# Attention over halves of 64 positions, two units per set, in front of two matrix products

## The chip, the cores and the metric

One core of a Trainium2 chip runs the kernel. TensorE multiplies matrices into PSUM (8 banks), VectorE (DVE), ScalarE (ACT) and GpSimd (POOL) work element by element, and SyncE (SP) issues transfers, as ACT and POOL can too. Each engine takes its instructions in the order of the program and waits at an instruction until its semaphores are there. The metric is the device time in microseconds (us), the median of several runs; the profile is one execution, taken by the hardware profiler.

## The reference, cut to what matters

```python
batch, n_heads, seq, head_dim = (4, 8, 768, 64)      # q, k, v, float32; lam: one decay rate per head
for b in range(nb):                                   # nb = 12 blocks of 64 positions
    intra = np.einsum('bhic,bhjc->bhij', qb, kb) * Dmask[None]      # lam ** (i - j) where i >= j
    intra = np.einsum('bhij,bhjd->bhid', intra, vb)
    inter = np.einsum('bhid,bhde->bhie', qb * lam_pow[None], kv_state)
    out[:, :, sl] = intra + inter
    kv_state = lam_block[None, :, None, None] * kv_state + np.einsum('bhsd,bhse->bhde', kb * rev_pow[None], vb)
x = out.transpose(0, 2, 1, 3).reshape(3072, 512)
h = x @ w_in                                          # 512 -> 2048
return (h * sigmoid(h)) @ w_out                       # 2048 -> 512
```

## The kernel before

The 3072 rows are 24 units of 128 positions: unit u is batch u // 6, block u % 6, and all 8 heads (4 pairs). Per unit there are three loads of 256 KB (k, q, v, in runs of 64 floats, 256 bytes). The first `EARLY = 8` units load all three plainly through SP's queue (line 313), cast k and q to bf16 on DVE or ACT (`cast`) and turn them with eight TensorE transposes (line 402) and a copy out of PSUM (`kqT`). The other sixteen load k and q by casting transfers that POOL issues (line 316) and turn them by a transposing transfer in SP's queue (line 416).

The attention of a unit on TensorE has four parts:

- `score` (line 427): per pair and head one matmul with 64 rows of contraction, 128 columns of weights and 128 columns streamed, over the whole 128 x 128 square of positions. DVE multiplies by a triangle on the way out of PSUM (`st`, two instructions).
- `state` (line 446): k times scaled v, 128 rows, 64 columns of weights, 64 columns streamed. DVE and POOL add the carried state and scale it (`y`, `xe`, `xf`).
- `out_mm` (line 481) with `xe` and `kqT`: the carried part, 64 x 64 weights per head, 128 columns streamed.
- `out_mm` with `vd` and `st`: the own part, 128 rows, 64 columns of weights, 128 columns streamed. DVE scales the sum by powers of lam into `xt` (bf16).

The powers of lam are split: v carries lam ** (64 - position), the result lam ** (position - 64), so that the mask is a plain triangle of ones.

`product1` (line 518) multiplies `w_in` by `xt` in groups of 1, 2 or 4 units, that is 128, 256 or 512 columns streamed, four matmuls for each of 16 column blocks; ACT applies the Silu from a full bank. `product2` (line 552) adds 16 matmuls of 512 columns per unit, or of 2 x 256 for the first six units and the last one. Results leave through ACT or DVE and ACT's queue.

The order on every engine comes from `Planner`: each piece of work is a task with a key, a cost per engine, dependencies and buffers; a simulated clock starts the ready task with the smallest key whose buffers are free. Each matmul pair is a task of its own, so products stand between the parts of a unit's attention. `BEGIN` says when each engine is taken to be free of its constants (POOL 3.4, ACT 6.0). The planner's times only decide the order that is written into the program; at run time the semaphores decide. Weights are loaded in eight pieces of 1 MB by POOL, and the order of the start is written out:

```python
    sequence = "u0 i0 i1 u1 i2 u2 i3 u3 u4 u5 u6 o0 o1 u7 o2 o3".split() + [f"u{u}" for u in range(EARLY, NU)]
```

Before a piece of weights POOL copies one element of the preceding unit's k (`gated`, line 293), and so waits for its landing.

Of the kernel before, what the change touches and what calls it, by code (L numbers as in the profile page):

```python
# [25 lines left out]
class Buf:  # L26

    __slots__ = ("pool", "slot", "left", "tile", "with_")

    def __init__(self, pool, with_=None):  # L30
        self.pool, self.slot, self.left, self.tile, self.with_ = pool, None, 0, None, with_

SMALL, CAST, LARGE, HALF, TURN = (256, 16.4, 18.5), (256, 14.0, 31.0), (2048, 92.0, 92.0), (1024, 58.0, 58.0), (1024, 46.0, 46.0)


class Planner:

# [17 lines left out]
    def order(self):  # L59
# [63 lines left out]
        while len(out) < len(self.tasks):  # L123
# [9 lines left out]
            for e in free:  # L133
# [7 lines left out]
                kept, took = [], None  # L141
                while ready[e]:
# [7 lines left out]
                    if any(len(self.pools[p]) < n for p, n in need.items()):  # L150
                        kept.append((key, i, t))
                        continue
# [37 lines left out]
def kernel(  # L190
# [20 lines left out]
    EARLY = 8  # L211
# [6 lines left out]
    POOLS = dict(bank=8, raw=9, rv=4, kq=6, kqT=5, vd=4, st=3, xe=3, y=3, xf=3,  # L218
                 xt1=4, xt2=2, xt4=2, g=40, osb=3, osh=4, one=4, two=2, att=5)
# [3 lines left out]
    def tile_of(b, shape, dt, name):  # L223
# [3 lines left out]
        return b.tile  # L227

# [18 lines left out]
    tri_e = const.tile([128, U], F32, name="tri_e")  # L247
    nc.gpsimd.memset(tri_e, 1.0)
    nc.gpsimd.affine_select(
        out=tri_e, in_=tri_e, compare_op=AL.is_ge, fill=0.0,  # L250
        base=0, pattern=[[1, U]], channel_multiplier=-1,
    )
# [12 lines left out]
    lam_be = const.tile([128, NP], F32, name="lam_be")  # L265
    nc.scalar.activation(lam_v, log_all, AF.Exp, scale=pose[:, 0:1])
    for a in range(NP):
        nc.scalar.activation(lam_xe[:, a, :], row, AF.Exp, scale=log_lam[:, a:a + 1])
    nc.scalar.activation(lam_be, log_lam, AF.Exp, scale=float(U))
    w_in_bf = const.tile([128, KI, DFF], BF16, name="w_in_bf")  # L270
# [12 lines left out]
    def mult(e, o, a, b):  # L283
        (nc.vector if e == "DVE" else nc.gpsimd).tensor_tensor(o, a, b, op=AL.mult)  # L284

    gate = const.tile([128, 8], F32, name="gate")

    def gated(key, load, i, tile):

        t = add(key, {"POOL": 0.15}, lambda e: nc.gpsimd.tensor_copy(gate[:, i:i + 1], tile()), deps=[load],  # L293
                prior=pool_last[-1:])
        pool_last.append(t)

    pool_last = []

    def pool_load(key, w, fn, bufs, nbytes, kind, late=0.0):
        t = add(key, {"POOL": w}, fn, bufs=bufs, nbytes=nbytes, kind=kind, prior=pool_last[-1:], late=late)  # L300
        pool_last.append(t)
        return t
# [309 lines left out]
```

## Time and profile before

| | |
|---|---|
| time, median of 3 runs | 233.99 us (233.22 to 235.63) |
| span of the profiled execution | 231.6 us, 2.4 us under the median |
| TensorE busy | 212.2 us, 92% |
| DVE, ACT, POOL busy | 89.4, 82.7, 41.3 us |
| first product matmul, first uninterrupted products | 16.8 us, 20.9 us |
| scores, states, outputs on the chain that ended last | 2.7%, 2.8%, 6.6% of the span |
| products on that chain | 38.3% and 35.7% |

The span runs from the first to the last instruction. The page's slices give the busy tenths of each engine in 40 equal parts of it; the chain that ended last is followed back from the last instruction to what released it; a group's line gives its count, busy time, the mean of one, and what ended the idle time before it. Matmuls overlap in the pipeline, so the mean of one (some 0.2 us) says little of its cost; the steps from one start to the next do, and the chain shows those.

### The profile page before, as it was taken

The numbers are of one execution on the slowest core, as the hardware profiler recorded it, in microseconds if no ns is written. First come the engines' busy times: TensorE is split into PE (matmuls) and PEld (weight loads), VectorE is DVE, ScalarE is ACT, GpSimd is POOL, SyncE is SP. The second block draws the span as 40 slices with busy tenths as digits, with TensorE's granted clock in tenths as the row PEclk, the third lists the DMA queues.
The fourth block names the chain that finished last, engine by engine and source line by source line (L and its number), as shares of the span: only waits on it lengthen the run. The fifth ranks groups of instructions, "written<-read, shape, count | busy, mean of one in ns | idle before, by whom it ended". The sixth has DMA issues, their size and how long they took to land.

```text
span 231.6 us, 4583 instructions
## 1 busy us (share of the span) xinstructions
PE 212.2 (92%) x1950; PEld 134.5 (58%) x1968; DVE 89.4 (39%) x165; ACT 82.7 (36%) x149; POOL 41.3 (18%) x61
## 2 busy tenths in 40 slices
PE   0547889999999999999999999999999999999994
PEld 0336778878888884686754444444444444444453
DVE  1445285766130007555574663556542111110100
ACT  5431625684433221242521146522323333333221
POOL 3403014922240003350333341011100000000000
PEclk9999979999999999999999999999999999999999
DMA  5999999999999985999999999610101111001112
GB/s 120 203 196 232 217 211 216 167 185 182 159 174 197 152 228 67 195 120 147 167 146 195 193 157 172 123 48 0 48 3 42 48 48 45 14 31 48 73 63 91
DMA packets 102677, 29.67 MB, mean 128 GB/s; under 512 B 92544, under 2 KB 100480, under 8 KB 102656
## 3 DMA queue, kind: packets, MB, share of 16 engines
q0 software_dynamic: 39552, 8.39, 41.3%
q1 hardware_dynamic: 58496, 14.68, 37.8%
q10 hardware_dynamic: 4608, 6.30, 7.9%
q8 instruction: 15, 0.25, 0.4%
q14 instruction: 6, 0.05, 0.1%
HBM read 27.27 MB, written 6.29 MB: 145 GB/s over the span
## 4 chain that ended last, share of the span: by engine, by line
PE 87%; DMA 6%; SPq 2%; DVE 1%; ACT 1%; issue 1%
PE h_ps L518 38%; PE o_ps L552 36%; PE x_ps L481 7%; DMA raw<-in_v_dram 6%; PE d_ps L446 3%; PE st_ps L427 3%; SPq L313 2%; PE tr L402 1%; DVE xt L284 1%; ACT g L532 0%; DVE vd L284 0%; ACT kqT L277 0%; ACT kq L277 0%; DVE xe L284 0%; DVE kqT L279 0%
## 5 line engine op out<-in xcount | busy, mean ns | idle before, releaser
L518 PE MATMUL h_ps<-xt,w_in_bf 128*128 128x128 bf16 (+2 forms) x700 | 115.9, 290 | 1.1 <-DVE xt L284 0.6
L552 PE MATMUL o_ps<-w_out_bf,g 128*128 128x512 bf16 (+1 forms) x482 | 105.4, 330 | 0.7 <-issue 0.5
L532 ACT ACTIVATE g<-h_ps 128x512 bf16<-128x512 f32 x96 | 56.6, 598 | 95.9 <-PE h_ps L518 91.6
L518 PEld LDWEIGHTS <-w_in_bf 128*128 128x128 bf16 x704 | 60.4, 102 | 27.0 <-issue 1.1
L552 PEld LDWEIGHTS <-g 128*128 128x128 bf16 x496 | 47.5, 98 | 32.3
L284 DVE TENSOR_TENSOR st<-st_ps,tri_e 128x512 bf16<-128x512 f32 x48 | 30.9, 685 | 32.1 <-PE st_ps L427 32.1
L279 DVE COPY osb<-o_ps 128x512 f32<-128x512 f32 (+1 forms) x11 | 6.8, 619 | 54.7 <-PE o_ps L552 53.0
L316 POOL DMA_DIRECT2D kq<-in_k_dram x16 | 14.1, 883 | 61.8 <-PE x_ps L481 56.3
L277 ACT ACTIVATE osb<-o_ps 128x256 f32<-128x256 f32 (+1 forms) x20 | 9.6, 479 | 36.0 <-PE o_ps L552 31.0
L284 DVE TENSOR_TENSOR xt<-x_ps,lam_xe 128x512 bf16<-128x512 f32 x24 | 16.5, 688 | 6.3 <-PE x_ps L481 5.9
L402 PE MATMUL tr<-ident,kq 128*128 128x128 bf16 x64 | 7.3, 242 | 11.4 <-POOL gate L293 5.7
L284 DVE TENSOR_TENSOR vd<-raw,lam_v 128x512 bf16<-128x512 f32 x24 | 16.2, 683 | 2.9 <-DMA raw<-in_v_dram 2.9
L316 POOL DMA_DIRECT2D kq<-in_q_dram x16 | 14.2, 890 | 7.3 <-DMA w_out_bf<-in_moe_w_out_dram 6.3
L458 DVE TENSOR_TENSOR y<-d_ps,xf 128x256 f32<-128x256 f32 x16 | 6.8, 425 | 18.5 <-PE d_ps L446 18.5
L277 ACT ACTIVATE kqT<-tr 128x512 bf16<-128x512 bf16 x14 | 8.4, 597 | 11.0 <-PE tr L402 10.9
L284 POOL TENSOR_TENSOR xf<-y,lam_be 128x256 f32<-128x256 f32 x6 | 3.7, 611 | 47.9 <-DVE y L458 47.9
L402 PEld LDWEIGHTS <-kq 128*128 128x128 bf16 x64 | 4.5, 106 | 12.6 <-DVE kq L279 9.3
L427 PE MATMUL st_ps<-kqT 64*128 64x128 bf16 x192 | 10.2, 229 | 1.6 <-ACT kqT L277 0.9
L481 PE MATMUL x_ps<-kqT,xe 64*64 64x128 bf16 x160 | 11.1, 231 | 0.0
L481 PE MATMUL x_ps<-st,vd 128*64 128x128 bf16 x192 | 11.0, 235 | 0.0
L427 PEld LDWEIGHTS <-kqT 64*128 64x128 bf16 x192 | 6.0, 98 | 8.4 <-issue 7.8
L446 PE MATMUL d_ps<-vd,kq 128*64 128x64 bf16 x160 | 9.0, 209 | 1.5 <-DVE vd L284 1.5
(32 smaller groups left out, 55.3 us busy)
## 6 DMA issues: line engine op xcount, KB each, us to landing
raw<-in_v_dram SPq DMA_DIRECT2D x24, 256.0 KB, 6.3
out_dram<-osb ACTq DMA_DIRECT2D x17, 256.0 KB, 2.1
raw<-in_k_dram SPq DMA_DIRECT2D x8, 256.0 KB, 4.9
raw<-in_q_dram SPq DMA_DIRECT2D x8, 256.0 KB, 6.2
w_in_bf<-in_moe_w_in_dram POOLq DMA_DIRECT2D x4, 512.0 KB, 8.0
w_out_bf<-in_moe_w_out_dram POOLq DMA_DIRECT2D x4, 512.0 KB, 13.8
kq<-in_k_dram POOLq DMA_DIRECT2D x16, 128.0 KB, 5.2
kq<-in_q_dram POOLq DMA_DIRECT2D x16, 128.0 KB, 6.5
```

The source lines that it names most:

```text
L277: nc.scalar.activation(o, i, AF.Copy)
L279: nc.vector.tensor_copy(o, i)
L284: (nc.vector if e == "DVE" else nc.gpsimd).tensor_tensor(o, a, b, op=AL.mult)
L316: nc.gpsimd.dma_start(out=tile_of(kq, [128, 2, H, 64], BF16, "kq")[:, i], in_=src[i])
L402: nc.tensor.transpose(t[:, m, :], kq_of()[:, i, 2 * m:2 * m + 2, :], ident)
L427: nc.tensor.matmul(t[:, m, :], lhsT=t_of()[r, 0, m, :], rhs=t_of()[r, 1, m, :], start=True, stop=True)
L446: nc.tensor.matmul(t[r, m, :], lhsT=kq_of()[:, 0, 2 * m + h, :], rhs=vd.tile[:, 2 * m + h, :], start=True, stop=True)
L458: nc.vector.tensor_tensor(tile_of(src, [128, NP, 64], F32, "y"), d_ps.tile, xf[0].tile, op=AL.add)
L481: nc.tensor.matmul(t[r, m, :], lhsT=lhsT(h, r), rhs=rhs(h, r), start=first, stop=True, skip_group_check=True)
L518: nc.tensor.matmul(t[:, j, :], lhsT=w_in_bf[:, ko, 128 * m:128 * m + 128], rhs=xt[gi].tile[:, ko, :], start=(ko == 0), stop=(ko == KI - 1))
L532: nc.scalar.activation(tile_of(g, [128, per, n], BF16, "g"), bank.tile, AF.Silu)
L552: nc.tensor.matmul(t, lhsT=g.tile[:, j, 128 * gp:128 * gp + 128], rhs=w_out_bf[:, ko, cs], start=(ko == 0), stop=(ko == KO - 1))
```

## The change

- Work goes by sets: two batches at the same block of 128 positions (`SETS`, 12 sets; unit u is now block u // 4, batch u % 4). Each load of a set is one transfer of 512 KB in SP's queue. No load is cast by POOL; all k and q are cast on DVE or ACT.
- The first two sets (`PAIRED`) are loaded with two neighbouring positions in a row of 64 partitions per batch, in runs of 512 bytes, and have code of their own (`prepare_2`, `first_2`, `second_2`) with masks `tri_2` and powers `lam_v2`. The first four sets are turned by TensorE, the other eight by one transposing transfer each.
- Inside a unit attention goes by halves of 64 positions: the scores of the two diagonal squares of 64 x 64 alone, two states (one per half, `mf` for the middle of the unit and `y` for its end) and a carried part for each half.
- Scores, states and own parts are all 64 x 64 matmuls that stream 64 columns. The state of a pair of heads is written into a 128 x 128 block diagonal (`xe_tiles`, six tiles filled with zeros at the start on POOL), so that the carried part is one matmul for both heads with 128 rows and 128 columns.
- From the fourth set on one TensorE task, `burst`, holds the first part of a set and the second part of the set before: states, outputs, scores, carried part, with no product between.
- The first products stream 256 columns (two groups per block in blocks 0 and 1), the others 512. A task of `product1` is now a whole bank, one of `product2` four matmuls.
- The planner keeps a later task from taking buffers that an earlier one lacks (`short`).

```diff
-    EARLY = 8
+
+    SETS = [[(0, 1), (2, 3)]] * 6
+    GROUPS = [[(0, 1), (2, 3)]] * 2 + [[(0, 1, 2, 3)]] * 4
+    PAIRED = 1
+    FRESH, TURNED, ALONE, LEAD = 4, 4, 3, 6.5
+    SEQUENCE = "s0 i0 i1 s1 i2 i3 s2 o0 o1 s3 o2 o3 s4"
+    POOLS = dict(bank=8, rk=4, rv=3, kq=3, kqT=3, vd=3, st=3, xe=6, xf=3, y=2, yf=2,
+                 xt2=3, xt4=2, g=40, osb=3, osh=4, one=3, two=2, att=6)
...
-                kept, took = [], None
+                kept, took, short = [], None, set()
...
-                    if any(len(self.pools[p]) < n for p, n in need.items()):
+                    lacks = {p for p, n in need.items() if len(self.pools[p]) < n}
+                    if lacks or short & set(need):
+                        short |= lacks
...
+    iota_2 = const.tile([128, 1], mybir.dt.int32, name="iota_2")
+    tri_2 = const.tile([128, 2, 2, 64], F32, name="tri_2")
+    nc.gpsimd.memset(tri_2, 1.0)
+    for r in halves:
+        nc.gpsimd.iota(iota_2[r], pattern=[[0, 1]], base=0, channel_multiplier=2)
+        for a in range(2):
+            for b in range(2):
+                nc.gpsimd.affine_select(
+                    out=tri_2[r, a, b], in_=tri_2[r, a, b], compare_op=AL.is_ge, fill=0.0,
+                    base=-1 if a > b else 0, pattern=[[1, 64]], channel_multiplier=-1,
+                )
+    pose_2 = const.tile([128, 2], F32, name="pose_2")
+    for a in range(2):
+        nc.vector.tensor_scalar(pose_2[:, a:a + 1], iota_2, -1.0, 64.0 - a, op0=AL.mult, op1=AL.add)
...
+    xe_tiles = [const.tile([128, 2, NP, 128], BF16, name=f"xe{i}") for i in range(POOLS["xe"])]
+    for t in xe_tiles:
+        nc.gpsimd.memset(t, 0.0)
...
+        if n < PAIRED:
+            def go_2(e, i, j):
+                t = tile_of(rk, [128, 2, H, 2, 64], F32, "rkq")[:, i] if i < 2 else tile_of(rv, [128, H, 2, 64], F32, "rv")
+                x = (k, q, v)[i][bs[0] + j, :, n * U:n * U + U, :].rearrange("h (p e) d -> p h (e d)", e=2)
+                nc.sync.dma_start(out=t[halves[j]].rearrange("p h e d -> p h (e d)"), in_=x)
+
+            for i in range(3):
+                ts.append([add((key, i), {"SP": 0.55}, lambda e, i=i, j=j: go_2(e, i, j), bufs=[rk if i < 2 else rv],
+                               nbytes=0.262, kind=WIDE, late=0.3) for j in range(2)])
+            raw[si] = rk, rv, ts
...
+            if last != unit:
+                rk, _, loads = raw[unit]
+                gated((m - 100, -1), loads[0], unit, lambda b=rk: b.tile[:, 0, 0, 0, 0:1] if len(b.tile.shape) == 5 else b.tile[:, 0, 0, 0:1])
                 last = unit
...
+        halves_of_d = [0, 1] if n < NB - 1 else [0]
+        st_ps = [Bank(fills=nb == 2) for _ in range(2)]
...
+        def states(e):
+            for j in range(nb):
+                for m in range(NP):
+                    for c in halves_of_d:
+                        r = halves[c]
+                        for p, rp in enumerate(halves):
+                            nc.tensor.matmul(d_of(c)[rp, j, m, :], lhsT=o.kq_of()[r, j, 0, m, p, :],
+                                             rhs=o.vd_of()[r, j, 2 * m + p, :],
+                                             start=j == 0 and m == 0, stop=True, skip_group_check=True)
+
+        def scores(e):
+            for j in range(nb):
+                for m in range(NP):
+                    for p, rp in enumerate(halves):
+                        t = tile_of(st_ps[p], [128, nb, NP, 64], F32, "st_ps")
+                        for c, r in enumerate(halves):
+                            nc.tensor.matmul(t[r, j, m, :], lhsT=o.kqT_of()[rp, j, 0, m, r], rhs=o.kqT_of()[rp, j, 1, m, r],
+                                             start=j == 0 and m == 0, stop=True, skip_group_check=True)
+
+        deps = o.turned + o.cv + [t for ts in o.ck for t in ts]
+        cost = 0.030 * 4 * nb * 2
+        return [states, scores], deps, st_ps + d_ps + [o.kqT, o.kq, o.vd], cost
...
+        def outs(e):
+            for j in range(nb):
+                for m in range(NP):
+                    for c, r in enumerate(halves):
+                        for h, rh in enumerate(halves):
+                            nc.tensor.matmul(x_of(c)[rh, j, m, :], lhsT=o.vd_of()[r, j, 2 * m + h, :],
+                                             rhs=o.st_of()[r, h, j, m, :],
+                                             start=j == 0 and m == 0, stop=True, skip_group_check=True)
+
+        def inter(e):
+            for c in range(2):
+                if n == 0 and c == 0:
+                    continue
+                for j in range(nb):
+                    for m in range(NP):
+                        nc.tensor.matmul(x_of(c)[:, j, m, :], lhsT=o.xe[c].tile[:, (bs[0] + j) % 2, m, :],
+                                         rhs=o.kqT_of()[:, j, 1, m, halves[c]],
+                                         start=False, stop=True, skip_group_check=True)
+
+        deps = o.masked + [t for t in o.xe_done if t]
+        return [outs, inter], deps, x_ps + [o.vd, o.st, o.kqT] + [b for b in o.xe if b], 0.030 * 4 * nb * (3 if n else 2)
...
+        order = [fs[1][0], fs[0][0], fs[1][1], fs[0][1]] if len(fs) == 2 else fs[0]
+
+        def go(e):
+            for f in order:
+                f(e)
+
+        t = add(key, {"PE": cost}, go, deps=deps, bufs=bufs)
+        after("b", t)
+        return t
+
...
+        def blocks(b, src, deps, bufs, i):
+
+            def go(e, r):
+                if b.tile is None:
+                    b.tile = xe_tiles[b.slot]
+                copy(e, b.tile[halves[r], b0:b0 + nb, :, halves[r]], src()[halves[r]])
+
+            return [add((s - 0.9, i), {"POOL": 0.25 + w / 1000, "ACT": 0.2 + w / 1200, "DVE": 0.1 + w / 1900}, lambda e, r=r: go(e, r),
+                        deps=deps, bufs=[b] + bufs) for r in range(2)]
...
+        elif si < ALONE:
+            after_first(o, burst((o.s - 0.5, 0), [first_part(o)]))
+            after_second(o, burst((o.s + 0.35, 0), [second_part(o)]))
+        else:
+            if open_ is None:
+                after_first(o, burst((o.s - 0.5, 0), [first_part(o)]))
+            else:
+                a, b = second_part(open_), first_part(o)
+                t = burst((o.s - 0.5, 0), [a, b])
+                after_second(open_, t)
+                after_first(o, t)
+            open_ = o
+    after_second(open_, burst((open_.s + 1.0, 0), [second_part(open_)]))
 
 
...
+            def mm(e, bank=bank, mg=mg):
                 t = tile_of(bank, [128, per, n], F32, "h_ps")
...
+                for j in range(per):
                     m = mg * per + j
...
+                    for ko in range(KI):
+                        nc.tensor.matmul(t[:, j, :], lhsT=w_in_bf[:, ko, 128 * m:128 * m + 128], rhs=xt[gi].tile[:, ko, :],
+                                         start=(ko == 0), stop=(ko == KI - 1))
```

In `after_first`, DVE masks both score banks (512 columns each), adds `d_ps` and the carried `xf` into `mf`, `d_ps` and `mf` into `y`, and DVE or POOL multiplies `y` by the rate into the next `xf`; `blocks` copies `mf` and `xf` into the block diagonals, 64 partitions at a time. In `after_second`, DVE scales each half's output into `xt`.

551 lines of the change are left out of this document (362 added, 189 removed).

## The prediction

> **What bounds the kernel now.** First the page's head and slices.
>
> ```profile
> span 231.6 us, 4583 instructions
> ...
> PE 212.2 (92%) x1950; PEld 134.5 (58%) x1968; DVE 89.4 (39%) x165; ACT 82.7 (36%) x149; POOL 41.3 (18%) x61
> ...
> PE   0547889999999999999999999999999999999994
> ...
> DMA  5999999999999985999999999610101111001112
> ```
>
> From the fifth slice on TensorE is full, the other engines are under half full, and the transfers are busy until about 150 us. So the time is the start plus all that TensorE does. The products are fixed: 196608 columns in each of the two, at 216 ns per 512 (the chain's "0.22" steps; 109 ns per 256, 56 ns per 128), are 166 us. The rest, some 65 us, is start, tail, attention and gaps. The chain of waits shows one unit's attention between products of 256 columns:
>
> ```profile
> 98.14 0.33 PE st_ps L427 x8
> 98.47 1.85 PE h_ps L518 x16
> 100.32 0.21 PE d_ps L446 x6
> 100.54 0.17 PE x_ps L481 x2
> 100.71 0.15 PE d_ps L446 x2
> 100.86 0.63 PE x_ps L481 x14
> 101.49 2.73 PE h_ps L518 x24
> ```
>
> Scores cost 0.33 us, and the 16 product steps after them 1.85 instead of 16 x 0.109 = 1.74: 0.11 more. States and outputs are 0.21 + 0.17 + 0.15 + 0.63 = 1.16, and the 24 steps behind them 2.73 instead of 2.62: again 0.11. One unit costs 0.44 + 1.27 = 1.7 us. How much of that is arithmetic? The busy time of narrow stretches, for line 446 and for line 481 alone, gives the starts (x counts the matmuls in flight in a stretch, so it grows by those that start):
>
> ```profile
> 100.25:100.28 0.03, 0.03 (x2) 1.00 0.75 68
> 100.28:100.30 0.02, 0.02 (x2) 1.00 0.19 38
> 100.30:100.33 0.03, 0.03 (x4) 1.00 0.29 60
> 100.33:100.36 0.03, 0.03 (x6) 1.00 0.26 60
> ...
> 101.07:101.13 0.06, 0.06 (x6) 1.00 0.17 30
> 101.13:101.19 0.06, 0.06 (x6) 1.00 0.08 19
> ```
>
> State matmuls (64 columns) start two at a time about every 29 ns, output matmuls (128 columns) two at a time every 56 ns: pieces that use different halves of the array run side by side. A unit is thus 4 x 56 (scores) + 4 x 29 (states) + 4 x 56 (carried part) + 4 x 56 (own part) = 0.79 us. The other 0.9 us is lost at changes of shape: product to scores and back, product to states, to carried part, back and forth, to outputs, to product, each 0.09 to 0.11 us.
>
> **What the change does to TensorE.** One set of two units becomes one burst: states, the previous set's outputs, scores (all in 64 x 64 pieces), then the carried part with all 128 rows and columns, which is the products' own shape. So two changes of shape per two units, not about sixteen. Slots of four 64-column pieces, one for each quarter of the array: 32 matmuls of states, 32 of outputs, 32 of scores are 24 slots. No four-quarter work is in the trace. Its floor is the 29 ns of a state pair, its ceiling two pairs in turn, 60 ns; I take 30, since the pairs already run both halves side by side and start 3 ns apart. The carried part has 16 matmuls of 64 columns with 128-column weights: between 29 ns (the state step) and 56 ns (the product step of 128 columns); I take 30, as it streams 64 columns. A burst is 24 x 30 + 16 x 30 + 2 x 0.1 = 1.4 us. Ten such sets and the separate bursts of set 2 and of the last outputs (0.4) are 14.4 us. A set loaded two positions per row has 8 slots of 64 columns and 16 of 128 and four bursts: 0.24 + 0.9 + 0.8 = 1.9; one of the two is behind the first product. Together 16.3. Before, 23 units at 1.7, less 0.35 for four without states and four without a carried part: 36.3. **Term one: -20.0 us.** Transposes stay 64 at 56 ns. Wider first groups (256 for 128, 512 for 256 columns) save 128 x (2 x 56 - 109) ns and as little again: **-0.5**.
>
> **The other engines.** Per two units DVE had scale 2 x 0.68, masks 4 x 0.69, y, xe, xf 6 x 0.42 and xt 2 x 0.69 = 8.0 us. Now: masks 2 x 0.69, two sums and one product of 512 columns 3 x 0.69, four block copies (nearest row: the 0.42 cast), four casts of 0.42 that the POOL transfers did before, scale and xt as before: 9.6 if DVE did all. TensorE needs 13.8 + 1.4 = 15.2 us per set, and DVE was busy 55 of 120 us from 60 to 180 us, ACT 38; ACT and POOL take copies too. Cost nothing, hidden by the 15.2 us of TensorE; without that cover it would be the 1.6 us per set more than before, 16 in all. What stays is that a burst waits for everything at once (casts, turns, the previous set's masks and blocks), with all products queued behind it: zero to 0.5 us each, I take 0.13, **+1.3** for ten.
>
> **Transfers.** POOL's casting loads vanish (41% of the engines' time); all of q, k, v come through SP's queue.
>
> ```profile
> 1.94 1.94 SPq L313 DMA_DIRECT2D raw<-in_v_dram  x1
> ...
> 5.23 0.44 POOL L293 COPY gate<-raw 128x1 f32<-128x1 f32 x1 [3.06 <-DMA raw<-in_k_dram]
> 5.61 1.70 POOL L333 DMA_DIRECT2D w_in_bf<-in_moe_w_in_dram  x2
> ...
> 133.88 13.25 SPq L416 DMA_TRANSPOSE kqT<-kq  x6
> ```
>
> In the SP rows of the timeline the undisturbed issues follow each other about every 1.15 us per 256 KB, and six turns take 13.25, 2.2 each. A set is 6 x 1.15 + 2 x 2.2 = 11.3 us of the queue against 15.2 of TensorE: supply outruns demand once the weights are in. The two first sets have 512-byte runs, the price of which is not shown: at worst 1.15 us per 256 KB, at best 0.8 (an estimate, about the pace of the weights' longer runs).
>
> **The start.** Before, the first 16 product steps come at 16.76 and continuous ones at 20.93, behind u1's v (issued 6.08, landed 19.4 among the weights). Now POOL first fills six block tiles of 1024 elements and makes ten small selects. From 0.10 us for one element and 0.20 for 128, a fill is 0.2 to 0.9; with ten selects at 0.2 to 0.3, POOL reaches its gate at 6 to 10.4 instead of 5.2, and the first w_in piece (5.9 us from issue to landing before) lands at 12 to 16. ACT has two more exponentials of 0.3 us (row lam_v) and DVE two ops of 0.15 (row pose) ahead of the first casts, behind which they waited for k and q anyway. Set 0 is undisturbed meanwhile: six loads land by 9 to 11, then casts, transposes, four masks (2.8 us of DVE), outputs and xt end at 16 to 18. Continuous products from 16.5 to 24, paced by w_in. DMA work until set 3 and w_out are in: four sets (25 us) and eight weight pieces of about 3.5 us (28), so near 55 us, with waits of 0 to 8 us for sets 2 and 3. I take 0 for the start and **+1.5** for these waits.
>
> Sum: 231.6 - 20.0 - 0.5 + 1.3 + 1.5 = 213.9 of span; the runs' median 233.99 stands 2.4 above the span, so 216.3, say **217**.
>
> **The rivals.** *All of the gain*: no waits at the bursts or for sets 2 and 3, and continuous products at 17, not 21: 216.3 - 2.8 - 4 = 210. For it: set 0 loads undisturbed. Against: POOL's late weights.
>
> *The start is paced by transfers*: w_in at 16, 20, 24, 28 us with TensorE still at half clock (before, 16 product steps of 128 columns took 1.89 us at 16.76, some 107 ns each, against 56 later), set 2 at 41, set 3 at 55; the 8 us of waits in full: 217 + 7 = 224.
>
> *Quarters run as pairs only*: 256 slots at 60, not 30, +7.7; 32 slots of 128 columns at 112, not 56, +1.8: 226. For it: no row with four at once.
>
> *Each piece takes a step of its own*: 4 x 29 and 4 x 56 ns per slot, +22 and +5: 244. Against it, two matmuls per 29 ns in the counts above, 14.5 ns each. The Trainium skill ("TensorE: Matmul & The Clock Gate", Part 1, "Wait — 56ns, not 53.3ns?") says that starts never come closer than about 25 ns however small the matmul; by that a slot would be 100 ns and the sum an estimated 18 us higher. The trace disagrees for pieces in different halves (29 ns per two).
>
> *SP's queue holds*, the slower side: it is served in order, and a turn waits for its casts. If a turn stands right behind its own set's loads, the loads after it wait for landing (v: 6.3 us in the page) and casts (two of 0.42 or 0.63), some 6.5 us per set. It decides from 15.2 - 11.3 = 3.9 us per set on; at 6.5 a set takes 17.8, eight sets from 60 us end at 202, where TensorE would want the last at 183: 217 + 19 + 2 = 238. Before, turns waited up to 2.9 us, and loads were three times fewer on that queue.
>
> **How the numbers follow.** Forecast 0.48 (211 to 222), all of the gain 0.17, start paced 0.13, pairs 0.10, queue holds 0.09, a step each 0.03. The measurement tells about 1% (2.3 us) from no change. Under 231.7 lie the first four less 0.03 for their upper ends: 0.85; over 236.3 the last, most of the fifth and a little of the fourth: 0.11; 0.04 between. The range goes from 207, below full gain, to 231, above pairs and the paced start together with some waiting; beyond it lie the queue and the single steps.
>
> **What would show it.** Right: chain share of d_ps, st_ps and x_ps from some 12% to 6 or 7%, bursts of 1.3 to 1.6 us on a critical path still 85% TensorE, four starts per 30 ns in narrow stretches; the first gate of POOL at 6 to 10 us; no software queue beyond the weights. Wrong: bursts of 2 us and more (pairs or single steps), TensorE slices under 9 after 60 us with waits on kqT (the queue), on st or xe (DVE, ACT or POOL late), or slices under 7 until 55 us (the start).

## The result and the profile after

| | before | after |
|---|---|---|
| median of 20 runs each | 233.6 us | 233.2 us |
| ratio to before, 95% interval | | 0.990 (0.987 to 0.993) |
| span of the profiled execution | 231.6 us | 229.6 us |
| TensorE busy | 212.2 us | 199.6 us |

The ratio leaves out the runs that lie more than 1.5% above the fastest of their kernel (nine of the 20 after), so it is not the quotient of the medians, which is 0.998. The change is 1% faster; the forecast was 7%, with a range that ended at 231. TensorE has 12.6 us less to do and the span is 2.0 us shorter: ten microseconds have become waiting. The head of the page after shows where (PE slices under 9 up to the twenty-fifth, where before all were 9 from the seventh on):

```profile
span 229.6 us, 5340 instructions
...
PE 199.6 (87%) x2339; PEld 122.8 (54%) x2352; DVE 90.1 (39%) x167; ACT 95.7 (42%) x173; POOL 33.3 (15%) x58
...
PE   0257885999999979979979895999999999999994
...
PE 65%; DMA 22%; DVE 7%; ACT 2%; issue 1%; SPq 1%; POOL 1%; DVEq 0%; POOLq 0%
```

The chain that ended last is 65% TensorE where the forecast had 85%; 22% of it is transfers. It holds this stretch (start, us, what):

```profile
87.90 0.38 PE d_ps L659 x32
88.28 0.26 PE x_ps L691 x32
88.54 0.27 PE st_ps L669 x32
88.81 0.57 PE x_ps L701 x16
...
92.06 7.89 DMA kqT<-kq
100.00 0.44 PE st_ps L669 x32
100.44 0.35 PE x_ps L701 x8
100.82 1.30 DVE xt L313 x2
102.16 0.39 PE h_ps L852
```

The first four lines are one burst, 1.48 us for two units. The next burst, from 98.8 on, holds set 5's second part and set 6's first part. Set 5's carried part (`x_ps` L701) stands behind set 6's scores, and these wait until set 6 is turned: issued at 92.06, landed at 100. Only then can `xt` of set 5 be made, and only then can the products of block 2 begin (sets 4 and 5 are its four units), the first with 512 columns: 102.2 us. TensorE itself stands still for only 1.6 us here (0.45 for the turn, 1.15 for `xt`), because other products fill the time until 98.8. The waits of TensorE from 60 to 150 us (us in total, times, longest) name the same places:

```profile
PE st_ps L669 <- DMA kqT<-kq: 3.4, 3, 2.4
PE h_ps L852 <- DVE xt L313: 2.3, 2, 1.2
```

The beginning, TensorE's rows (start, us, what, and in brackets the idle time before):

```profile
20.33 3.60 PE L852 MATMUL h_ps<-xt,w_in_bf 128*128 128x256 bf16 x16 [1.64 <-DMA w_in_bf<-in_moe_w_in_dram]
24.64 3.59 PE L852 MATMUL h_ps<-xt,w_in_bf 128*128 128x256 bf16 x16 [0.71 <-DMA w_in_bf<-in_moe_w_in_dram]
...
31.44 1.92 PE L852 MATMUL h_ps<-xt,w_in_bf 128*128 128x256 bf16 x16 [0.81 <-DMA w_in_bf<-in_moe_w_in_dram]
...
40.65 6.05 PE L852 MATMUL h_ps<-xt,w_in_bf 128*128 128x256 bf16 x32 [1.06 <-DVE xt L313]
```

The weights land piece by piece, the first at 20.3, the last at 31.4. Sixteen matmuls take 3.60 us at 20.33 and 1.92 at 31.44: the first run at half speed, and so do most of those from 40.65. For the second stretch the records show a granted clock of 0.5 (38.8 to 45.6); for the first they show no such entry, so that a half clock is there only inferred from the steps. By 60 us products worth 21.7 us have started, before it was 23.5. (Each matmul on record counts with its step at full speed, scaled so that all make 166.2 us, because a few records are missing; such figures, here and below, are good to about 1 us.)

**Where the time is.** If the trace's steps from one TensorE start to the next are added up by kind, and split where the products of blocks 0 and 1 (a third of all, 55.4 of 166.2 us) are done, this comes out. In the kernel before, that point is at 95.0 us; after, it is block 2's first product at 102.2; the last TensorE instruction ends at 228.5 and 226.1.

| us | before, to 95.0 | after, to 102.2 | before, from there | after, from there |
|---|---|---|---|---|
| no matmul in flight | 15.2 | 21.6 | 1.2 | 5.0 |
| products | 59.6 | 62.4 | 114.0 | 110.6 |
| attention | 14.7 | 11.6 | 18.3 | 8.5 |
| transposes | 5.7 | 6.5 | 0 | 0 |

Behind block 2's start the change gains 9.5 us (133.5 to 124.0, 3.8 more idle time included); ahead of it 7.2 are lost. Cut at 60 us instead, the time without a matmul is 15.0 before and 18.8 after up to there, and 1.3 before and 7.8 after from there on.

### The profile page after: what moved, and what is told of

Read it like the earlier page. It is cut to its first block, busy times and chain, and to the rows that moved or that the text cites. A ratio compares the mean times of both kernels' runs of the same rounds, so it can differ in the third digit from the quotient of the medians.

```text
span 229.6 us, 5340 instructions
## 1 busy us (share of the span) xinstructions
PE 199.6 (87%) x2339; PEld 122.8 (54%) x2352; DVE 90.1 (39%) x167; ACT 95.7 (42%) x173; POOL 33.3 (15%) x58
## 4 chain that ended last, share of the span: by engine, by line
PE 65%; DMA 22%; DVE 7%; ACT 2%; issue 1%; SPq 1%; POOL 1%; DVEq 0%; POOLq 0%
PE o_ps L886 31%; PE h_ps L852 28%; DMA rkq<-in_k_dram 9%; DMA kqT<-kq 6%; DMA w_in_bf<-in_moe_w_in_dram 6%; PE x_ps L701 2%; DVE xt L313 2%; DVE kq L308 1%; PE st_ps L669 1%; DVE st L313 1%; DVE vd L313 1%; PE tr L451 1%; PE d_ps L659 1%; PE x_ps L691 1%; DVE xf L313 1%
## 5 line engine op out<-in xcount | busy, mean ns | idle before, releaser
L852 PE MATMUL h_ps<-xt,w_in_bf 128*128 128x256 bf16 (+1 forms) x506 | 98.5, 341 | 6.8 <-DVE xt L313 3.4
L886 PE MATMUL o_ps<-w_out_bf,g 128*128 128x512 bf16 (+1 forms) x489 | 91.3, 330 | 0.4
L852 PEld LDWEIGHTS <-w_in_bf 128*128 128x128 bf16 x512 | 52.0, 103 | 42.4 <-DMA w_in_bf<-in_moe_w_in_dram 4.2
L306 ACT ACTIVATE osb<-o_ps 128x512 f32<-128x512 f32 (+1 forms) x26 | 13.4, 514 | 28.5 <-PE o_ps L886 28.5
L313 POOL TENSOR_TENSOR vd<-rv,lam_v 128x512 bf16<-128x512 f32 x12 | 13.1, 1101 | 80.8 <-DMA rv<-in_v_dram 72.2
L313 DVE TENSOR_TENSOR xt<-x_ps,lam_xe 128x512 bf16<-128x512 f32 x24 | 15.6, 693 | 21.8 <-PE x_ps L701 19.2
L313 DVE TENSOR_TENSOR st<-st_ps,tri 128x512 bf16<-128x512 f32 x28 | 17.9, 683 | 3.4 <-PE st_ps L669 2.7
L308 DVE CAST kq<-rkq 128x512 bf16<-128x512 f32 x28 | 12.9, 480 | 10.8 <-DMA rkq<-in_k_dram 7.1
L306 ACT ACTIVATE kq<-rkq 128x512 bf16<-128x512 f32 x20 | 12.4, 626 | 10.9 <-DMA rkq<-in_k_dram 7.0
L308 DVE CAST xe<-yf 64x512 bf16<-64x512 f32 x16 | 9.8, 612 | 0.4
L313 DVE TENSOR_TENSOR vd<-rv,lam_v 128x512 bf16<-128x512 f32 x12 | 8.0, 684 | 2.5 <-DMA rv<-in_v_dram 2.5
```

The costliest lines, as they stand in the source:

```text
L306: nc.scalar.activation(o, i, AF.Copy)
L308: nc.vector.tensor_copy(o, i)
L852: nc.tensor.matmul(t[:, j, :], lhsT=w_in_bf[:, ko, 128 * m:128 * m + 128], rhs=xt[gi].tile[:, ko, :], start=(ko == 0), stop=(ko == KI - 1))
L886: nc.tensor.matmul(t, lhsT=g.tile[:, j, 128 * gp:128 * gp + 128], rhs=w_out_bf[:, ko, cs], start=(ko == 0), stop=(ko == KO - 1))
```

## The experiments

All are edits of the kernel after, but for one; ratios are to the kernel before (the change: 0.990). "Block 2" is the start of its first product, 102.2 in the change, and "rest" the time from there to TensorE's end, 124.0, with 5.0 us idle. An edit of an order, a set or a planner's figure lets the planner lay out every engine anew, transfers included.

**Fills of the block tiles on DVE instead of POOL.**

```diff
-        nc.gpsimd.memset(t, 0.0)
+        nc.vector.memset(t, 0.0)
```


> The change, with the six block tiles filled with zeros on DVE instead of POOL; nothing else moves. Theory A (the start): the fills hold POOL until 10.8 us, so w_in lands at 20 to 31 us and TensorE, bound to the written order, does set 1's attention late and at half clock; POOL's gate should now come near 5 us, w_in land 5 us earlier, and the time fall by 4 to 8 us, to a ratio of 0.955 to 0.975. Theory B (supply): the transfers are busy without a break until 147 us and give one set per 11 us, so TensorE waits at the bursts for what it wins at the start: ratio 0.985 to 0.995, and the idle time of TensorE between 60 and 150 us grows from 7 us to 10 or more.

0.993 (0.989 to 0.997); first product at 19.5 instead of 20.3, 22.1 us of products by 60 us, block 2 at 102.3. POOL's gate came at 6.82 instead of 10.79 us (5.95 of that were the six fills) and `w_in` landed 2 to 3 us earlier, less than the 5 expected; the first product waits for `xt` now. A gate 4 us earlier gains nothing, so POOL's late gate by itself is not what costs the time. Theory B's ratio is met, but not its idle time, which fell from 7.4 to 6.2.

**The same fills put into the kernel before.**

```diff
+    fill = [const.tile([128, 1024], BF16, name=f"fill{i}") for i in range(6)]
+    for t in fill:
+        nc.gpsimd.memset(t, 0.0)
```


> The kernel before, with six fills of 128 x 1024 on POOL ahead of its first gate, into tiles that nothing reads: POOL's gate goes from 5.2 to about 8 us, w_in 3 us later. Theory A: TensorE's products start 1 to 3 us later and the time grows as much: ratio 1.005 to 1.013. Theory B: the engines' transfers are as busy as ever, u1 and u2 come earlier instead: 0.998 to 1.004.

0.991 (0.988 to 0.994): faster, against the expectation. The first three pieces of `w_in` land 2 us later, the last 2 us earlier; the first product comes at 14.7 instead of 16.8, and 24.6 us of products have started by 60 us. Later weights leave the first units' loads more room, which would explain it, but this was not tried by itself; what the run shows is that the fills do no harm.

**Fewer bytes in the later sets, then in the first four.** One of 16 heads of q is loaded, k is cast in its place.

```diff
-                nc.sync.dma_start(out=t[:, i], in_=src[i])
+                if i == 1 and si >= FRESH:          # in the second run: si < FRESH, and go_2 likewise
+                    nc.sync.dma_start(out=t[:, i, 0:1], in_=src[i][:, 0:1])
+                else:
+                    nc.sync.dma_start(out=t[:, i], in_=src[i])
```


> The change, with q's transfers of sets 4 to 11 cut to one of 16 heads, and k cast in q's place, so that the scores are of k with k: same order, some 4 MB less through SP's queue. Theory A: the start is untouched, only the bursts' waits for turned sets go: up to 7 us of TensorE's idle time between 60 and 150 us, ratio 0.96 to 0.98. Theory B: the same wait is all that stands between the change and its gain in this stretch, ratio 0.96 or below. Third theory (the bursts wait for DVE, ACT or POOL): no change, 0.985 to 0.995, the waits stay.

0.967 (0.964 to 0.970). Block 2 still at 101.7, but idle time behind it 0.0 and the rest 119.2: fewer bytes take away the waits at the later bursts, not the late start of block 2.

> The change, with q's transfers of sets 0 to 3 cut to one head per batch and k cast in q's place (scores of k with k): same order, about 1.9 MB less before 60 us. If the first 60 us are paced by what lands (theory B, now for the start), products done by 60 us grow from 21.7 us worth by 4 to 8 and the time falls by 4 to 8 us: ratio 0.955 to 0.975. If TensorE's written order and the chains of casts and masks pace it, less than 2 us: 0.982 to 0.992.

0.986 (0.982 to 0.991), the same as the change within the intervals. First product 20.1, 22.9 us by 60 us. The start is not paced by the bytes of q in these four sets.

**The planner's figures set to what the trace shows** (gate of POOL 10.8; a turn 2.2 us per unit and not half of that; 512-byte runs slower); then the figure for the turn alone.

```diff
-..., WIDE, ..., TURN = ..., (512, 25.0, 27.0), ..., (1024, 46.0, 46.0)
+..., WIDE, ..., TURN = ..., (512, 45.0, 45.0), ..., (1024, 92.0, 92.0)
-    BEGIN = {"PE": 0.8, "ACT": 6.0, "DVE": 2.7, "POOL": 3.4, "SP": 0.8}
+    BEGIN = {"PE": 0.8, "ACT": 6.0, "DVE": 2.7, "POOL": 10.8, "SP": 0.8}
```


> The change, with three of the planner's figures as this profile has them: POOL free at 10.8 instead of 3.4 us, 45 ns instead of 25 for a 512-byte packet, 92 instead of 46 for 1024 bytes of a turn. Work and transfers are the same, only the order differs. Theory A: set 1's attention goes ahead of the products that wait for w_in, the bursts come when their turned sets are there: 4 to 8 us less, ratio 0.955 to 0.975. Theory B: order doesn't bring sets sooner: 0.985 to 0.995.

0.975 (0.970 to 0.979), block 2 at 102.2, idle time behind it 0.0, rest 120.5.

> The change with one planner figure altered, 92 instead of 46 ns per 1024 bytes of a turning transfer; the start's order should hardly move. If the bursts' waits for turned sets are a loss by themselves, TensorE's idle time between 60 and 150 us falls from 7.4 to 4 or less and the ratio is 0.973 to 0.982. If the gain of the true figures came from the start: 0.985 to 0.995, idle as before.

0.972 (0.966 to 0.977), block 2 at 102.1, idle 0.7, rest 120.7. The waits for turned keys from 60 to 150 us, 3.4 in the change, are now

```profile
PE st_ps L669 <- DMA kqT<-kq: 0.9, 1, 0.9
```

One number in the planner is worth 2%: with the turn taken at half its time, bursts stood in the program ahead of the landing of their turned keys, and all products behind them waited. The one wait that is left is that of the burst ahead of block 2 (turn issued at 91.98, landed at 99.92), and block 2's start does not move.

**No rows of two positions,** alone and with the planner's figures.

```diff
-    PAIRED = 1
+    PAIRED = 0
```


> The change, with the first two sets loaded like the others (256-byte runs over 128 partitions, two loads' worth per transfer) and taken through the common code. If the 512-byte runs into 64 partitions are what makes the start slow (45 ns a packet in the change, where two of 256 bytes take 36), sets 0 and 1 land some 2 us earlier and the time falls by 1 to 3 us: ratio to the kernel before 0.977 to 0.987. If the start is set by the sum of sets and weights that must land before set 1's products, 1 us or less: 0.985 to 0.995; the four separate bursts and the shorter chain of this form may add to either.

0.989 (0.985 to 0.993).

> The change with the first two sets loaded like the others, and the planner's figures for POOL's start (10.8) and for turns (92) as measured. If the two losses (attention of the first sets in a long chain of its own form; bursts ahead of their turned sets) are separate, the gains of unpaired (0.989) and of the true figures (0.975) add up against the change's 0.990: ratio 0.968 to 0.977. If what is won by 60 us is waited for again at the bursts, as with set 1 first: 0.975 to 0.99.

0.972 (0.967 to 0.978), as with the figure alone. Loading the first sets two positions per row is worth nothing that can be measured.

**Set 1 loaded ahead of the weights,** alone and with the planner's figures.

```diff
-    SEQUENCE = "s0 i0 i1 s1 i2 i3 s2 o0 o1 s3 o2 o3 s4"
+    SEQUENCE = "s0 s1 i0 i1 i2 i3 s2 o0 o1 s3 o2 o3 s4"
```


> The change, with set 1's loads ahead of the first weights in the order of the start (s0 s1 i0 i1 i2 i3 s2 ...), so that POOL's first gate waits for set 1's k. The bytes are the same. If what paces the start is that set 1 shares the engines with 4 MB of weights while only one group's products can run, set 1's attention now ends before w_in is complete, both groups run as w_in lands, products done by 40 us go from 7 to 12 or more and the time falls by 3 to 7 us: 0.96 to 0.98. If the sum of bytes decides, nothing is won by 60 us: 0.985 to 0.995.

1.030 (1.027 to 1.033), outside both ranges. 25.8 us of products by 60 us, 4 more than the change, but the transfers are then less busy (share 0.69 from 60 to 80 us, 1.19 in the change), TensorE waits 6.3 us for a set of block 1 until 65.8 and 5.9 us for the turned keys of the joined burst ahead of block 2, which starts at 112.4: a gain of 4 at the start, a loss of 10 at block 2.

> Set 1's loads ahead of the weights, and the planner's three figures as measured. If the start (order of arrival) and the bursts' waits (order against late turns) are two losses that don't make up for each other, the gains of the two edits add: 0.950 to 0.965. If supply limits both, the second gives back what the first wins: 0.97 to 0.98, as with the figures alone.

1.001 (0.998 to 1.004): the figures take back 3%, where they gave 1.5% to the change itself; the ratio is outside both ranges. Since the order moved two things at once, this pair does not price the start by itself.

**An early start: one unit in each of sets 0 and 1,** with the fills on POOL, then on DVE; both without rows of two positions and with the planner's turn at 92 (POOL's gate at 10.8, then 5.0).

```diff
-    SETS = [[(0, 1), (2, 3)]] * 6
+    SETS = [[(0,), (1,), (2, 3)]] + [[(0, 1), (2, 3)]] * 5
...                                  # GROUPS likewise
-    PAIRED = 1
+    PAIRED = 0
...                                  # FRESH, TURNED, ALONE = 5, 5, 4; two buffers fewer for g
-    SEQUENCE = "s0 i0 i1 s1 i2 i3 s2 o0 o1 s3 o2 o3 s4"
+    SEQUENCE = "s0 i0 i1 s1 i2 s2 i3 s3 o0 o1 s4 o2 o3 s5"
```


> As the version with unpaired first sets and the two planner figures, but the first two units are sets of one unit with products of 128 columns, each followed by a piece or two of w_in; two fewer buffers for g make room. If two units per set are what delays the start (the first product waits for both units' loads), the first product comes at 15 to 17 us instead of 19 to 20, products done by 60 us grow by 2 or more, and the ratio is 0.955 to 0.970. If the start is paced by bytes and by TensorE's order, no gain over the two-unit form: 0.97 to 0.98 or worse, by two more sets' bursts (0.2 us each).

0.962 (0.955 to 0.969); first product 19.2, 24.4 us by 60 us, block 2 at 103.3. (These three are from an execution of 228.8 us; the run's fastest took 223.4.)

> As the version whose first two units are sets of one, with the block tiles filled on DVE and the planner's POOL start at 5.0 instead of 10.8: both of what stands ahead of the first product, two units' loads and the late weights, are gone at once. If these two together made the late start, the first product comes at 14 to 17 us, products done by 60 us grow by 2 to 4 us worth over the 24.4 there, and the ratio is 0.945 to 0.957. If earlier weights only take the engines from the sets, first product at 17 or later and ratio 0.957 to 0.970.

0.976 (0.970 to 0.982), no better than with the figure for the turn alone (0.972), and above both ranges. This is the cleanest single test of the forecast's start:

```profile
12.92 1.86 PE L852 MATMUL h_ps<-xt,w_in_bf 128*128 128x128 bf16 x16
...
79.75 0.64 PE L669 MATMUL st_ps<-kqT 64*64 64x64 bf16 x32 [5.00 <-DMA kqT<-kq]
...
82.31 6.61 PE L852 MATMUL h_ps<-xt,w_in_bf 128*128 128x256 bf16 x40 [0.95 <-DVE xt L313]
...
103.84 0.61 PE L852 MATMUL h_ps<-xt,w_in_bf 128*128 128x512 bf16 x1 [1.15 <-DVE xt L313]
```

Products begin at 12.9 and 29.1 us of them have started by 60. That is about what the forecast's sum meant for the start: no less than the 23.5 of before, and some of the saved attention on top. At 80 us it is 42.8, where the change has 42.0: a joined burst has waited 5.0 us for turned keys. The granted clock is 0.5 from 76.4 to 86.6, so that the 40 matmuls behind that wait take 6.61 us, where the change needs 4.54, and block 2 starts at 103.8. The whole gain of 7.4 us is given back before block 2. So the late start was real, but undoing it alone does not move the end.

**Twice the small matmuls:** states, scores and outputs of sets 2 to 11 are issued twice.

```diff
+            for again in range(2):
...
-                                             start=j == 0 and m == 0, stop=True, skip_group_check=True)
+                                             start=not again and j == 0 and m == 0, stop=True, skip_group_check=True)
```


> The change with the states, scores and outputs of sets 2 to 11 issued twice (the second pass adds to the first, so that these parts come out doubled); the order is the same. By the trace each pass is 0.27 us per part and set: 0.8 us per set, 8 us in all more work inside the bursts. If TensorE's own time sets the end from 45 us on, the time grows by 5 to 8 us (8 less what the waits behind it take in): ratio 1.012 to 1.025. If transfers set it, by 2 us or less: 0.99 to 1.0.

1.131 (1.123 to 1.138), far outside. The chain shows that the pieces themselves cost what was said, and that TensorE then stops without a wait that the profile shows (`issue`):

```profile
83.17 0.64 PE d_ps L660 x64
83.81 0.53 PE x_ps L694 x64
84.34 0.12 PE st_ps L671 x15
84.47 3.06 issue
87.53 0.86 PE st_ps L671 x29
```

64 states in 0.64, 64 outputs in 0.53: 8 to 10 ns a piece (in the change 8 to 12). The waits of TensorE over the whole run say how much the stops are:

```profile
PE st_ps L671 <- issue: 21.5, 7, 4.0
```

21.5 of the 35.9 us that the span grew in this execution (267.2 us; the run's fastest took 263.1). Behind the stops the granted clock is 0.5 for 27.3 us in all (in the change for 6.8, ahead of 60 us). In each of the seven stops a transfer of 16 KB in the queue for instructions begins between 0.5 us before the stop and 1.9 us into it (at 84.8 in the one above); this speaks for instructions that come too slowly, which was not tested by itself. As a price of the bursts the run says nothing beyond the 8 to 10 ns.

**Separate bursts:** each set's first and second part stand alone, with products between.

```diff
-    FRESH, TURNED, ALONE, LEAD = 4, 4, 3, 6.5
+    FRESH, TURNED, ALONE, LEAD = 4, 4, 12, 6.5
```


> The change with each set's two parts as bursts of their own (two changes of shape more per set, 8 sets, 0.2 us each: 1.6 us more for TensorE), so that the outputs of one set no longer wait behind the states and scores of the next. If the waits at joined bursts cost more than they save, TensorE's idle time from 60 to 150 us falls from 7.4 by 3 or more and the ratio is 0.975 to 0.988; if the joining is sound and only the late turns hold the bursts, 0.992 to 1.002.

0.967 (0.963 to 0.971), more than either theory gave. TensorE's rows at the place of the joined burst, and SP's row of set 6's turn:

```profile
89.47 4.07 PE L887 MATMUL o_ps<-w_out_bf,g 128*128 128x256 bf16 x23
93.47 0.45 PE L691 MATMUL x_ps<-st,vd 64*64 64x64 bf16 x32
93.85 0.64 PE L701 MATMUL x_ps<-kqT,xe 128*128 128x64 bf16 x16
94.54 2.54 PE L887 MATMUL o_ps<-w_out_bf,g 128*128 128x512 bf16 x11
96.92 3.62 PE L853 MATMUL h_ps<-xt,w_in_bf 128*128 128x512 bf16 x16
...
87.41 6.40 SPq L634 DMA_TRANSPOSE kqT<-kq  x1
```

Set 5's carried part runs at 93.85 and not behind set 6's keys, which land at 97.8 here; products cover the time in which DVE makes `xt`, and block 2 starts at 96.9, five earlier, with 2.0 us idle behind it. Not all of the five is gain: between 60 us and block 2 TensorE's idle time falls from 2.8 to 0.1 us, while 1.8 us of attention and 1.0 of products now stand behind block 2's start. From 60 us on it falls from 7.8 to 2.1 us in all. The joining of bursts, which saves two changes of shape per set, costs more than it saves, as this order has it; the new order also issues set 6's turn 4.6 us earlier, and no run parts the two.

**More products behind block 2's start:** the first of the four matmuls of each bank is issued twice in blocks 2 and 3.

```diff
-                    for ko in range(KI):
+                    for first, ko in ([(True, 0)] if n0 in (2, 3) else []) + [(False, ko) for ko in range(KI)]:
...
-                                         start=(ko == 0), stop=(ko == KI - 1))
+                                         start=(ko == 0), stop=(first or ko == KI - 1))
```


> The first of the four matmuls of each bank in blocks 2 and 3 is issued twice: 32 more product matmuls of 512 columns, at 0.216 us 6.9 us more of TensorE, all of it behind the first product of 512 columns at 102 us. Theory (the end is the start of block 2's products, plus TensorE's own 120.5 us from there, plus idle time at bursts; the change has about 5 us of idle time behind 102 us): the start of block 2 stays at 102 and the time grows by 6.9 less what the longer products hide of the 5 us, so by 3 to 7 us; against the kernel before 1.003 to 1.02 (the change: 0.990). Rival (the end is set by the arrival of later sets, TensorE has slack behind 102 us): by 2 us at most, ratio under 1.0.

1.003 (1.000 to 1.007), span 233.0, 3.4 us more. Block 2 at 101.9, the rest 127.6 with 0.6 us idle: 6.9 us of work came in and hid 4.4 us of waiting, and a granted clock of 0.5 for 3.4 us from 102.5 on, which the change does not have there, adds to the rest. From block 2's start on, TensorE's own work sets the end, and the idle time at the bursts is what could be had there.

**Separate bursts with the early start; separate bursts with the figure for the turn.**

The first run has `ALONE = 13`, the edits of the early start on DVE and the turn at 92; the second has `ALONE = 12` and the turn at 92.

> The early start (sets 0 and 1 of one pair of units each, block tiles filled on DVE) together with separate bursts for every set. With joined bursts the early start gave 29 us of products done by 60 us and all of it was back at 80 us (ratio 0.976). Theory (the joined burst holds set 5's outputs behind set 6's turned keys, so that block 2's products begin at 102 us however early the start was): without the joining the first product of 512 columns comes at 88 to 95 us, the time is that plus 120.5 plus 2 to 5 idle plus 3.4 to the end of the span, 215 to 223, ratio 0.925 to 0.955. Rival (block 2 is bound by the arrival of set 5 through SP's queue, joined or not): first product of 512 columns at 96 to 98 us as with separate bursts alone, ratio 0.96 to 0.97.

0.967 (0.964 to 0.971). 28.0 us of products by 60 us, 46.7 by 80, but block 2 at 97.3: the rival's number, and no better than separate bursts alone.

> The change with separate bursts for every set, and with the planner's figure for a turn at the measured 92 ns per KB (2.2 us per 256 KB is about this). Each alone gave a ratio of 0.967 and 0.972. If they act on different things (the separate bursts on the start of block 2's products, 102 to 97 us; the figure on the idle time at later bursts, 5 us to 1): first product of 512 columns at 97, idle time behind it under 1 us, 0.955 to 0.962. If both take away the same wait: 0.964 to 0.972.

**0.960 (0.956 to 0.965)**, the best of all, span 223.4. Block 2 at 99.1, idle behind it 1.2, rest 120.8. The ratio is in the first theory's range, but the two gains don't add up (that would be 0.949), and the trace says that both edits take away largely the same waits: from 60 us on TensorE is idle for 7.8 us in the change, 3.9 with the figure, 2.1 with separate bursts and 1.5 with both. The rest of what this run gains over separate bursts lies ahead of 60 us (18.6 us idle for 20.8), at which neither edit was aimed. Against the first run it shows that the early start wins nothing on top of the other two edits.

**Fewer bytes in the first of these two** (one head of q in blocks 2 to 5, as above; block 2 has sets 5 and 6 here, because block 0 is three sets).

> The early start and separate bursts, and in the sets of blocks 2 to 5 only one of 16 heads of q is loaded, with k cast in its place (q is left out there). The two sets of block 2 are 0.98 MB less, 4.8 us of transfers at 205 GB/s. Theory (with the early start and the separate bursts TensorE has run out of other products at 95 us, and block 2 waits for the arrival of its second set through the transfers): first product of 512 columns at 91 to 94 us instead of 97.3, time 219 to 222, ratio 0.94 to 0.955 (without the cut 0.967). Rival (what holds block 2 there is the chain of casts, turns and masks behind the landing, or TensorE itself): 96 to 98 us, ratio 0.96 to 0.97.

0.967 (0.959 to 0.976), block 2 at 96.9: the arrival theory falls. The chain of this run shows what stands there instead:

```profile
91.05 0.37 PE d_ps L662 x32
91.42 0.33 PE st_ps L672 x32
91.76 1.27 DVE st L313 x2
93.03 0.61 DVE yf L313
...
93.66 0.42 DVE xe L308
94.08 0.60 DVE y L313
...
95.54 1.28 DVE xt L313 x2
...
96.86 0.38 PE h_ps L856
```

The states and scores of block 2's second set (set 6 here) stand behind nearly all of block 1's products in the program, though its turn was issued at 76.6 and had landed at 82.5. Once they have run at 91.7, three product matmuls are left to cover 5 us of DVE's masks, states, block copies and `xt`. In this order it is the written place, not the transfer. An order that puts this set earlier was not tried.

## Why the prediction was wrong

**What held.** The pieces: a burst takes 1.48 us (forecast 1.4). Narrow stretches of line 659 show three or four starts per 30 ns (x counts those in flight):

```profile
80.72:80.75 0.03, 0.03 (x10) 1.00 1.23 316
80.75:80.78 0.03, 0.03 (x14) 1.00 1.15 299
80.78:80.81 0.03, 0.03 (x17) 1.00 0.98 299
80.81:80.84 0.03, 0.03 (x21) 1.00 1.05 273
```

The single starts of these states come in fours, 3 ns apart, and 32 ns lie from one four to the next: 8 ns a piece, and 32 for the slot that the forecast took at 30. So both rivals of slower pieces fall. The Trainium skill's rule ("TensorE: Matmul & The Clock Gate", Part 1, "Wait — 56ns, not 53.3ns?": no two starts closer than about 25 ns) differs from these rows, and the measurement decides for pieces in four quarters of the array; for pieces in one and the same quarter, 32 ns apart, it does not contradict the rule. POOL's gate at 10.79 was just above the upper bound of 10.4, and POOL's software queue carries only weights. One reading of the forecast was wrong without weight in the sum: the 41% of the engines' time in that queue were POOL's casting loads and the weights together; with the weights alone it is 12%, so the loads were some 29%.

**What failed, by the terms of the sum.** The forecast's span was 213.9, the measured one 229.6.

- *Term one with the wider groups,* -20.5: measured -12.7 (the three rows with matmuls in the table, 212.3 to 199.6). Attention before was 33.0, and 3.4 more in product steps at changes of shape (114.0 against 110.6 behind block 2's start), 36.4 (forecast 36.3). After it is 20.1 (forecast 16.3): ten bursts at 1.48 are 0.8 of that difference, the rest, about 3 by difference, lies with the first sets, whose bursts stand alone and run partly at half clock. Products ahead of block 2 cost 2.8 more, where 0.5 less was forecast, and transposes 0.8 more; the half clock lasts longer there (64 matmuls from 20.3 and 40.7 on took 13.2 us, at full speed 7.0), and the sum had no term for this. Together 7.8 short.
- *Start 0 and waits for sets 2 and 3 +1.5:* time without a matmul until 60 us, 15.0 to 18.8, +3.8 (2.1 of it until the first matmul). 2.3 short.
- *Waits at bursts +1.3:* time without a matmul from 60 us on, 1.3 to 7.8, +6.5. 5.2 short.

With 0.4 more from TensorE's end to the end of the span, 213.9 + 7.8 + 2.3 + 5.2 + 0.4 = 229.6. The third is the step that failed in kind, and the one that the experiments show: from 60 us on the idle time falls from 7.8 to 3.9 us with the figure for the turn, to 2.3 with fewer bytes in the later sets and to 2.1 with separate bursts. I priced a burst's wait as 0.13 us, a mean over ten, and it measured some 0.65; a burst queues everything behind it, and it waits for the latest of two sets. "SP's queue holds", the rival nearest to this, had a chance of 0.09 and a price of 21 us; the sign that it named, slices under 9 after 60 us with waits on `kqT`, came, but at three bursts only and for 3.4 us, because the turn landed behind the burst's place in the program. The queue as a whole did not hold: a new order alone takes most of these waits away. "The start is paced by transfers" came true in its signs, some 3 us later than it said (weights landing at 20, 25, 28, 31; half speed), but the early start shows that undoing it gains nothing while block 2 waits. The price of a joined burst and that of a start must be read at the next thing that consumes them: the products of block 2, of which the forecast had no line.

Two edits undo parts of this: against the change, the figure for the turn gives -1.9%, separate bursts -2.4%, both -3.0%. What remains between the best kernel's 223.4 and the 213.9 is, by the table alone, the half clock, the first sets' bursts and the idle time ahead of block 2 (18.9 us in the best kernel, 15.2 before). No run kept the clock up or made the first sets' bursts cheaper, so how much each of these is worth in time stays open.

## What to carry to other kernels

Work saved on the bounding engine can be lost again at the next point where that engine runs out of work; find these points (here the joined bursts, and the first product that needs two more sets) and write down when their inputs arrive, before adding up savings. Joining two pieces of work into one uninterrupted task makes the earlier one wait for the inputs of the later one: here two changes of shape of 0.1 us per set were saved, and with separate bursts TensorE was idle for 5.7 us less from 60 us on. Where a planner writes the order, its cost figures are part of the kernel; one figure off by a factor of two cost more than the change won.

## What the runs showed of the hardware

- Small matmuls in the four quarters of the array started 8 ns apart on average in the change (fours 32 ns apart), yet in the doubled bursts TensorE stopped seven times for 21.5 us together, after 111 to 187 pieces in a row (64 + 64 + 15 = 143 in the lines above). The change, with 96 such pieces in a row, shows no such stop.
- After a stretch with gaps TensorE's clock was granted at 0.5 for 6.8 us (38.8 to 45.6) in the change, for 3.4 us in the kernel before (31.0 to 34.4) and for 10.2 us with the early start (76.4 to 86.6), so that the products behind a gap are slower as well. The Trainium skill ("TensorE: Matmul & The Clock Gate", Part 1) states windows of about 3.4 us after which the clock follows the activity; two, one and three such windows agree with the traces.
- A turn of a set took 5.7 to 8.3 us from issue to landing in the change, with loads under way (7.9 in the chain at 92.06); a turn of one unit in the kernel before took 5.3 in the median, and six of them issued in a row held SP's queue for 13.25 us.
- A fill of 128 x 1024 bf16 elements on POOL took 0.99 us (5.95 for six).
